# The first group's hidden activations: split where they are made, spilled in two parts, reloaded by transfers alone

## Chip, cores and metric

One core of a Trainium2 chip runs the whole program in one launch. The metric is the device time of one execution in microseconds (us); lower is better. Before the change it was measured in three runs.

## What is computed

Three layers in a row, all in float32:

```python
scores = scale * np.matmul(q, k.transpose(0, 1, 3, 2))   # 4 x 8 heads, 768 positions, 64 wide; sinks and a window of 128
a = softmax(np.where(keep, scores, -1e9))
x = np.matmul(a, v)                                      # laid out as 3072 tokens x 512
h = np.maximum(np.maximum(x @ w1, x @ w2), x @ w3)       # 512 -> 768
x2 = h @ w_out                                           # 768 -> 512
logits = x2 @ w_gate                                     # 8 experts, 384 tokens each, assigned by rank
out[mask] = np.maximum(x2[mask] @ u1[e], 0.0) @ u2[e]    # for each expert e
```

## The kernel before

TensorE gets its accuracy from splitting every float32 operand in a high part (a rounded copy, written by ScalarE) and a low part (operand minus high part, by VectorE or GpSimd), and from three products high x high, low x high, high x low. A split of one 128x384 tile is thus one ScalarE copy and one VectorE subtraction.

The 3072 tokens go through in eight groups of 384. For each group four attention units (`att`, p = 0 to 3) give the tiles `x` (128x384 each). `Moe1.group` (L260) splits them into `xh0..3`, `xl0..3` (L267, L268; one buffer each), multiplies by the three weights (L280, 36 products for each of six blocks f), takes the maximum into `hm` (L282 ScalarE, L283 VectorE; two buffers), and splits `hm` (L288, L289) into the parts of one tile `HL` (`part`, six high and six low). `Moe1.x2` (L294) multiplies H by the output weight, six accumulations of 18 products (L305), evicts (L307) and stores x2d.

The first group is an exception. When its H is made, the output weight `woh`, `wol` does not exist yet: `load_out` (L240) makes it during the second group, from six 512 KB words tiles that `single` (L214) loads into the ring `st` of the pool `conv` (two buffers), and the space of `HL` is still the landing ring of the first weights. So the first group stores `hm` itself, unsplit, into `sp` in DRAM (L285, on ScalarE's queue), and after the second group's `x2`, `reload` (L317) loads each `hm` again on SyncE's queue (L321), splits it (L323 ScalarE, L324 VectorE) into `HL`, and a second `x2` follows at once.

Program order is: group 0; group 1; x2 of group 1; reload; x2 of group 0; group 2, and so on. Attention of the coming groups is woven in at high priority, so between 177 and 233 us the engines run the two `x2` and the attention of groups 2 and 3 side by side. A scheduler that simulates the engines decides the final order on each queue; every queue then runs in order. For attention of those groups ScalarE copies keys and queries (`kh`, `qs`), evicts scores (`T`), takes exponentials (L144), rounds the probabilities (`H`, L176); VectorE does the low parts (`kz`, `qs`: L95, L97), masks (L135) and the split maxima and products; GpSimd scales (`T`, L147) and makes the low part of the probabilities (`L`, L177). Groups 0 and 1 use a simpler attention without these splits (`native`), but during group 0 the first weights are unpacked and split, on GpSimd above all (L228, L213).

Of the kernel before, what the change touches and what calls it, by code (L numbers as in the profile page):

```python
# [19 lines left out]
FT=mybir.dt.float32; FR=mybir.dt.float32r; BF=mybir.dt.bfloat16; I32=mybir.dt.int32; U8=mybir.dt.uint8; U32=mybir.dt.uint32  # L20
AF=mybir.ActivationFunctionType; OP=mybir.AluOpType; AX=mybir.AxisListType
NEG=-8.0e9
def f32(ap): return ap.bitcast(FT)
# [179 lines left out]
class Moe1:  # L203
# [56 lines left out]
    def group(s,xs,spill=None,pool=None,mid=None,between=None):  # L260

        nc=s.nc; main=s.main
        X=[]
        for p in range(4):
            h=main.tile([128,384],FR,name=f"xh{p}",bufs=1); l=main.tile([128,384],FR,name=f"xl{p}",bufs=1)
            with s.tc.high_priority():
                nc.scalar.activation(h,xs[p],AF.Copy)  # L267
                nc.vector.tensor_tensor(l,xs[p],f32(h),op=OP.subtract)  # L268
            X.append((h,l))
        H=[]  # L270
        if s.HL is None and spill is None: s.HL=main.tile([128,12,384],FR,name="HL")
        for f in range(6):
            if between is not None: between(f)
            m=main.tile([128,384],FT,name="hm",bufs=2)
            for i in range(3):
                ps=s.mm.tile([128,512],FT,name="mm")
                n=0
                for p in range(4):
                    for a,b in ((0,0),(0,1),(1,0)):
                        nc.tensor.matmul(ps[:,:384],s.W[i][a][:,p,f*128:(f+1)*128],X[p][b],start=(n==0),stop=(n==11)); n+=1  # L280
                with s.tc.high_priority():
                    if i==0: nc.scalar.activation(m,ps[:,:384],AF.Copy)  # L282
                    else: nc.vector.tensor_tensor(m,ps[:,:384],m,op=OP.max)  # L283
                if mid is not None and (f,i)==s.at: mid()
            if s.HL is None: nc.scalar.dma_start(spill[f],m); continue  # L285
            h,l=(pool.tile([128,384],FR,name=f"h{x}{f}",bufs=1) if pool else s.part(x,f) for x in "hl")
            with s.tc.high_priority():
                nc.scalar.activation(h,m,AF.Copy)  # L288
                nc.vector.tensor_tensor(l,m,f32(h),op=OP.subtract)  # L289
            if spill is not None:  # L290
                for d,x in zip(spill[f],(h,l)): nc.scalar.dma_start(d,f32(x))
            H.append((h,l))
        return H
# [21 lines left out]
                nc.scalar.activation(LG[:,t0+t,:].rearrange("p (u e) -> p u e",u=2),e,AF.Copy)  # L315
            nc.scalar.dma_start(x2d[(t0+t)*128:(t0+t+1)*128,:],o)
    def reload(s,spill):  # L317
        nc=s.nc; H=[]
        for f in range(6):
            m=s.main.tile([128,384],FT,name="hm",bufs=2)  # L320
            nc.sync.dma_start(m,spill[f])  # L321
            h,l=s.part("h",f),s.part("l",f)
            nc.scalar.activation(h,m,AF.Copy)  # L323
            nc.vector.tensor_tensor(l,m,f32(h),op=OP.subtract)  # L324
            H.append((h,l))
        return H
    def by_rows(s,spill,t0,x2d,accs,pool):

# [28 lines left out]
class Route:  # L357
# [4 lines left out]
    M=128  # L362
# [261 lines left out]
def attention_mixtures(tc,q,k,v,vs,words,wg,u1,u2,out,off=60,spread=(0,1,3,4),native=8,order='a0 a0 a0 a0 w a1 w a1 w w a1 w w a1 a2',order1='a2 o o o o o o a2 a2',back=1,at=(1,0),s1=300,s2=400,nring=6):  # L624
    nc=tc.nc
    PS=bass.MemoryType.PSUM
    with ExitStack() as ctx:
# [6 lines left out]
        x2d=dram.tile([3072,512],FT,name="x2d")  # L634
        A=Attn(tc,q,k,v,vs,consts,ac,pst,psp,pss,psv,work)
        M=Moe1(tc,words,wg,consts,wpool,main,conv,mm,pst,pss,A.ident)
        M.at=at
        LG=consts.tile([128,24,8],FT,name="LG")
        NG=8; xs={}; cnt={}
# [7 lines left out]
        with tc.block(schedule_with_timeline_sim=True):  # L647
# [16 lines left out]
            rest=None  # L664
            for g in range(NG):
                if g==1:
                    for o in order1.split(): emit(o,True)
                late=list(range(cnt.get(f'a{g+1}',-1)+1,4)) if g+1<NG else []
                def between(f):
                    if f in spread and late: late.pop(0); emit(f'a{g+1}',True)  # L670
                if g<2:
                    while late: between(spread[0])
                d = g>=NG-3
                if g==0: sp=[dram.tile([128,384],FT,name=f"sp{f}") for f in range(6)]
                if g==NG-3: sp2=[[dram.tile([128,384],FT,name=f"sp{f}{x}") for x in "hl"] for f in range(6)]
                if g==NG-1:
                    A.extra.release(); work.release(); ac.release(); psv.release(); pss.release(); psp.release()
                    acc=P("acc",1,space=PS); rc=P("rc",2,space=PS)
                    rt=P("rt",1); rw=P("rw",2); hp=A_("hp",1)
                    r=Route(tc,LG,rt,rw,rc)  # L680
                H6,H=H if g==NG-1 else None,M.group(xs[g],sp if g==0 else sp2 if g==NG-3 else None,hp if g==NG-1 else None,rest,between)
                while late: between(spread[0])
                rest=None
                if d:
                    rest=M.logits(H,3*g,LG)
                    if g==NG-1: r.bids((0,21),True)
                elif g: M.x2(H,3*g,LG,x2d)
                if g==back:
                    M.x2(M.reload(sp),0,LG,x2d)
# [30 lines left out]
            P7=[main.tile([128,384],FR,name=f"x{j}") for j in range(3)]  # L720
            for j in range(3): nc.vector.tensor_scalar(P7[j],io,r.q[:,T7+j:T7+j+1],None,op0=OP.is_equal)
        M.x2(H6,T7-3,LG,x2d,256,hp)
        M.by_rows(sp2,T7-6,x2d,acc,hp)
        with tc.high_priority(): fet(0)
        M.x2(H,T7,LG,x2d,256,hp,keep)
        hp.release()
# [62 lines left out]
```

## Time and profile before

| what | before |
|---|---|
| median of 3 runs (lowest to highest) | 992.21 us (989.67 to 995.44) |
| the profiled execution's own time | 988.75 us |
| its span | 986.9 us |
| TensorE busy (PE, share of the span) | 933.9 us (95%) |
| VectorE (DVE) / ScalarE (ACT) / GpSimd (POOL) busy | 687.5 / 534.4 / 349.0 us |

Engines are called as the profile calls them: PE is TensorE's matmuls, PEld its weight loads, DVE VectorE, ACT ScalarE, POOL GpSimd, SPq and ACTq the queues on which SyncE and ScalarE issue transfers. L305 is line 305 of the kernel before. A busy time counts the instructions of an engine, not the issue of transfers. "a <-b" behind an idle time names what ended it.

### The profile page before, as it was taken

The numbers are of one execution on the slowest core, as the hardware profiler recorded it, in microseconds if no ns is written. First come the engines' busy times: TensorE is split into PE (matmuls) and PEld (weight loads), VectorE is DVE, ScalarE is ACT, GpSimd is POOL, SyncE is SP. The second block draws the span as 40 slices with busy tenths as digits, with TensorE's granted clock in tenths as the row PEclk, the third lists the DMA queues.
The fourth block names the chain that finished last, engine by engine and source line by source line (L and its number), as shares of the span: only waits on it lengthen the run. The fifth ranks groups of instructions, "written<-read, shape, count | busy, mean of one in ns | idle before, by whom it ended". The sixth has DMA issues, their size and how long they took to land.

```text
span 986.9 us, 18459 instructions
## 1 busy us (share of the span) xinstructions
PE 933.9 (95%) x6552; PEld 853.2 (86%) x6552; DVE 687.5 (70%) x1807; ACT 534.4 (54%) x1425; POOL 349.0 (35%) x317
## 2 busy tenths in 40 slices
PE   5889999979999999999999999999999999999996
PEld 3569889969999999999999998888888888878895
DVE  4887766797889875766755335978988879774320
ACT  5766765888789786777663211333433424335431
POOL 3689256056446526415442000001303113043331
PEclk9999999979999999999999999999999999999999
DMA  7554122222112112112110002634534243454430
GB/s 231 166 187 141 50 76 67 86 91 66 39 57 83 48 34 69 40 48 88 60 44 2 1 1 87 193 112 129 164 98 168 100 158 127 136 184 145 137 107 32
DMA packets 50541, 95.03 MB, mean 96 GB/s; under 512 B 6704, under 2 KB 20784, under 8 KB 50448
## 3 DMA queue, kind: packets, MB, share of 16 engines
q1 hardware_dynamic: 40560, 71.57, 23.5%
q0 software_dynamic: 3840, 12.45, 3.6%
q10 hardware_dynamic: 6048, 9.83, 2.7%
q8 instruction: 51, 0.84, 0.4%
q14 instruction: 42, 0.34, 0.1%
HBM read 77.84 MB, written 16.12 MB: 95 GB/s over the span
## 4 chain that ended last, share of the span: by engine, by line
PE 72%; DVE 9%; issue 6%; ACT 6%; DMA 4%; POOL 2%; SPq 0%; POOLq 0%; ACTq 0%; DVEq 0%
PE mm L280 28%; PE mm L608 10%; PE acc L601 10%; PE mm L305 6%; PE po L181 3%; PE rc L406 2%; DMA sa<-in_u_dram 2%; PE pt L25 2%; PE pp L25 2%; PE po L172 1%; PE acc L336 1%; PE ps L126 1%; PE ps L127 1%; PE ps L123 1%; DVE qs L97 1%
## 5 line engine op out<-in xcount | busy, mean ns | idle before, releaser
L601 PE MATMUL acc<-wbh,HL 128*128 128x512 f32 x384 | 131.8, 400 | 0.8 <-issue 0.8
L177 POOL TENSOR_TENSOR L<-A_w,H 128x768 fp32r<-128x768 f32 x46 | 87.1, 1894 | 101.8 <-ACT H L176 95.8
L283 DVE TENSOR_TENSOR hm<-mm,hm 128x384 f32<-128x384 f32 x96 | 53.3, 555 | 68.6 <-PE mm L280 64.1
L620 POOL DMA_INDIRECT out_dram<-og,idx x24 | 31.8, 1323 | 185.8 <-ACT og L619 182.4
L305 PE MATMUL mm<-woh,HL 128*128 128x260 f32 (+1 forms) x432 | 88.2, 293 | 2.0 <-DVE HL L324 1.1
L552 ACT ACTIVATE wah<-sa 128x512 fp32r<-128x512 f32 x64 | 40.4, 632 | 89.0 <-PE mm L608 56.3
L601 PEld LDWEIGHTS acc<-wbh,HL 128*128 128x128 f32 x384 | 71.7, 189 | 14.4 <-DVE qi L520 1.3
L552 ACT ACTIVATE wbh<-sb 128x512 fp32r<-128x512 f32 x64 | 40.3, 630 | 72.4 <-PE acc L601 56.5
L601 PE MATMUL acc<-wbl,HL 128*128 128x512 f32 x192 | 77.0, 401 | 0.0
L305 PEld LDWEIGHTS mm<-woh,HL 128*128 128x128 f32 x432 | 71.1, 195 | 3.4 <-DVE HL L324 1.4
L608 PE MATMUL mm<-HL,wah 128*128 128x384 f32 x256 | 68.5, 343 | 0.0
L280 PE MATMUL mm<-xh,w0h 128*128 128x384 f32 x192 | 66.8, 348 | 1.3 <-ACT xh L267 0.6
L553 DVE TENSOR_TENSOR wbl<-sb,wbh 128x512 fp32r<-128x512 f32 x64 | 44.8, 701 | 33.0 <-ACT wbh L552 30.0
L280 PE MATMUL mm<-xh,w1h 128*128 128x384 f32 x192 | 66.8, 348 | 0.8 <-ACT hm L282 0.5
L280 PE MATMUL mm<-xl,w0h 128*128 128x384 f32 x192 | 65.5, 341 | 1.9 <-DVE xl L268 1.9
L280 PE MATMUL mm<-xh,w2h 128*128 128x384 f32 x192 | 66.4, 346 | 0.2 <-ACT hm L282 0.2
L280 PE MATMUL mm<-xh,w1l 128*128 128x384 f32 x192 | 65.3, 340 | 0.0
L280 PE MATMUL mm<-xh,w0l 128*128 128x384 f32 x192 | 65.2, 339 | 0.0
L280 PE MATMUL mm<-xl,w2h 128*128 128x384 f32 x192 | 65.1, 339 | 0.0
L280 PE MATMUL mm<-xl,w1h 128*128 128x384 f32 x192 | 65.0, 339 | 0.0
L280 PE MATMUL mm<-xh,w2l 128*128 128x384 f32 x192 | 64.8, 337 | 0.0
L612 DVE SCALAR_TENSOR_TENSOR HL<-mm,HL 128x384 fp32r<-128x384 f32 x64 | 35.4, 553 | 39.5 <-ACT HL L611 39.4
(320 smaller groups left out, 2877.2 us busy)
## 6 DMA issues: line engine op xcount, KB each, us to landing
sa<-in_u_dram SPq DMA_DIRECT2D x64, 256.0 KB
sb<-in_u_dram SPq DMA_DIRECT2D x64, 256.0 KB
HL<-in_words_dram SPq DMA_DIRECT2D x18, 512.0 KB
qn<-in_q_dram SPq DMA_DIRECT2D x24, 192.0 KB
x2d<-xo ACTq DMA_DIRECT2D x15, 256.0 KB
kn<-in_k_dram SPq DMA_DIRECT2D x12, 264.0 KB
st<-in_words_dram SPq DMA_DIRECT2D x6, 512.0 KB
vn<-in_v_dram SPq DMA_DIRECT2D x12, 256.0 KB
```

The costliest lines, as they stand in the source:

```text
L25: nc.tensor.transpose(out,x,f32(ident))
L177: nc.gpsimd.tensor_tensor(L,Af,f32(H),op=OP.subtract)
L181: nc.tensor.matmul(po[:,q:q+n],u['VS'][:,blk,128*h:128*h+128],part[:,c:c+n],start=(part is H and j==0),stop=False,skip_group_check=True)
L280: nc.tensor.matmul(ps[:,:384],s.W[i][a][:,p,f*128:(f+1)*128],X[p][b],start=(n==0),stop=(n==11)); n+=1
L283: else: nc.vector.tensor_tensor(m,ps[:,:384],m,op=OP.max)
L305: nc.tensor.matmul(ps[:,:n],H[f][a][:,t*128:(t+1)*128],s.WO[b][:,f,u,c],start=(k==0),stop=(k==17)); k+=1
L552: nc.scalar.activation(h,src,AF.Copy)
L553: (nc.gpsimd if s.n>=6 and nm=="wa" else nc.vector).tensor_tensor(l,src,f32(h),op=OP.subtract)
L601: s.mms.append(nc.tensor.matmul(acc[t],H[f][a][:,t*128:(t+1)*128],W[f][1][b],start=(f==0 and n==0),stop=(f==F-1 and n==2))); n+=1
L608: s.mms.append(nc.tensor.matmul(ps[:,:384],W[f][0][a][:,k,:],X[k][b],start=(n==0),stop=(n==11))); n+=1
L612: nc.vector.scalar_tensor_tensor(l,ps[:,:384],0.0,f32(h),op0=OP.max,op1=OP.subtract)
L620: st=nc.gpsimd.indirect_dma_start(out=s.out,out_offset=bass.IndirectOffsetOnAxis(ap=idx[:,t:t+1],axis=0),in_=o,in_offset=None)
```

## The change

The first group's H is split like that of the others, into a tile `hp` that takes turns in the ring `st` of `conv` (the same two buffers that the output weight's words land in later), and both parts are stored. `reload` has no ScalarE or VectorE work left: it loads high and low part of blocks 0 to 3 into the tiles `xh0..3`, `xl0..3`, and blocks 4 and 5 into their parts of `HL`.

```diff
@@ Moe1.group
-            if s.HL is None: nc.scalar.dma_start(spill[f],m); continue
-            h,l=(pool.tile([128,384],FR,name=f"h{x}{f}",bufs=1) if pool else s.part(x,f) for x in "hl")
+            if s.HL is None: h,l=(s.conv.tile([128,2,384],FR,name="hp",tag="st",bufs=2)[:,x] for x in range(2))
+            else: h,l=(pool.tile([128,384],FR,name=f"h{x}{f}",bufs=1) if pool else s.part(x,f) for x in "hl")
             with s.tc.high_priority():
                 nc.scalar.activation(h,m,AF.Copy)
                 nc.vector.tensor_tensor(l,m,f32(h),op=OP.subtract)
@@ Moe1.reload
-        nc=s.nc; H=[]
+        H=[]
         for f in range(6):
-            m=s.main.tile([128,384],FT,name="hm",bufs=2)
-            nc.sync.dma_start(m,spill[f])
-            h,l=s.part("h",f),s.part("l",f)
-            nc.scalar.activation(h,m,AF.Copy)
-            nc.vector.tensor_tensor(l,m,f32(h),op=OP.subtract)
-            H.append((h,l))
+            H.append([s.main.tile([128,384],FR,name=f"x{x}{f}",bufs=1) if f<4 else s.part(x,f) for x in "hl"])
+            for d,x in zip(spill[f],H[f]): s.nc.sync.dma_start(f32(x),d)
         return H
@@ attention_mixtures
-                if g==0: sp=[dram.tile([128,384],FT,name=f"sp{f}") for f in range(6)]
-                if g==NG-3: sp2=[[dram.tile([128,384],FT,name=f"sp{f}{x}") for x in "hl"] for f in range(6)]
+                if g in (0,NG-3): sp=[[dram.tile([128,384],FT,name=f"sp{g}{f}{x}") for x in "hl"] for f in range(6)]
```

The stores of both parts are the lines that stood at L290 and L291 already, on ScalarE's queue. (The sixth group's spill, `sp2` before, is only renamed.)

The scheduler then orders every queue anew. TensorE's queue where the two `x2` meet, before (`HL` is group 0's H from the first L305 here on; `kh_x`, `kz0b` are keys of group 3's attention, whose scores go to `ps`):

```order
L182 MATMUL po<-psb_105,vk_103 128x384
L126 MATMUL ps<-kh_x,qs_2602 128x260
L127 MATMUL ps<-kz1b,qs_2602 128x260
L126 MATMUL ps<-kh_x,qs_2601 128x260
L127 MATMUL ps<-kz0b,qs_2601 128x260
L305 MATMUL mm<-woh,HL 128x260
L305 MATMUL mm<-wol,HL 128x260
L305 MATMUL mm<-woh,HL 128x260
L305 MATMUL mm<-wol,HL 128x260
```

and with the change:

```order
L182 MATMUL po<-psb_105,vk_103 128x384
L126 MATMUL ps<-kh_x,qs_2634 128x260
L127 MATMUL ps<-kz1b,qs_2634 128x260
L305 MATMUL mm<-woh,xh_2291 128x260
L305 MATMUL mm<-wol,xh_2291 128x260
L305 MATMUL mm<-woh,xl_2292 128x260
L305 MATMUL mm<-woh,xh_2295 128x260
L305 MATMUL mm<-wol,xh_2295 128x260
L305 MATMUL mm<-woh,xl_2296 128x260
L305 MATMUL mm<-woh,xh_2299 128x260
```

One pair of scores has moved behind the start of group 0's `x2`, which now reads the tiles `xh`, `xl`; its first twelve products are those of blocks 0 to 3.

ScalarE's queue where group 2's x is split. Before, the first two splits (`xh_2408`, `xh_2412`) stand right behind the second group's last evictions (L282), ahead of both `x2`:

```order
L282 ACTIVATE hm<-mm 128x384
L134 ACTIVATE T_w<-ps 128x132
L256 ACTIVATE wgt<-ps 128x8
L267 ACTIVATE xh_2408<-x_986 128x384
L267 ACTIVATE xh_2412<-x_1391 128x384
L134 ACTIVATE T_w<-ps 128x132
L288 ACTIVATE HL<-hm 128x384
```

With the change they stand at the very end of group 0's `x2`, of whose twelve evictions (L307) those shown are the last two:

```order
L307 ACTIVATE xo<-mm 128x260
L144 ACTIVATE T_w,l<-T_w,m 128x132 x2
L267 ACTIVATE xh_2440<-x_986 128x384
L144 ACTIVATE T_w,l<-T_w,m 128x132 x3
L176 ACTIVATE H<-A_w 128x768
L144 ACTIVATE T_w,l<-T_w,m 128x132
L108 ACTIVATE vsp<-vn 128x4x2x64
L183 ACTIVATE x_1828<-po 64x384
L267 ACTIVATE xh_2444<-x_1427 128x384
L267 ACTIVATE xh_2448<-x_1708 128x384
L307 ACTIVATE xo<-mm 128x260
```

All four splits of group 2's x now come after the products that read the reloaded H out of the same tiles.

SyncE's queue at the reload, before and with the change:

```order
L75 DMA kn<-in_k_dram 128x528
L321 DMA hm<-sp_1032 128x384
L321 DMA hm<-sp_1033 128x384
L75 DMA kn<-in_k_dram 128x528
L77 DMA qn<-in_q_dram 128x384
L75 DMA kn<-in_k_dram 128x528
L77 DMA qn<-in_q_dram 128x384
L321 DMA hm<-sp_1034 128x384
L321 DMA hm<-sp_1035 128x384
```

```order
L321 DMA xh_2303<-sp03h 128x384
L321 DMA xl_2304<-sp03l 128x384
L75 DMA kn<-in_k_dram 128x528
L77 DMA qn<-in_q_dram 128x384
L75 DMA kn<-in_k_dram 128x528
L77 DMA qn<-in_q_dram 128x384
L321 DMA HL<-sp04h 128x384
L321 DMA HL<-sp04l 128x384
L321 DMA HL<-sp05h 128x384
L321 DMA HL<-sp05l 128x384
```

Eight transfers now come in one row ahead of the next keys, and the last four, which need the parts of `HL` that the second group's `x2` reads to its end, stand where the third and fourth transfer stood.

## Rows read from the trace of the kernel before

**Rows 1.** The page: span, busy time of each engine, PE's busy tenths in 40 slices.

```profile
span 986.9 us, 18459 instructions
...
PE 933.9 (95%) x6552; PEld 853.2 (86%) x6552; DVE 687.5 (70%) x1807; ACT 534.4 (54%) x1425; POOL 349.0 (35%) x317
...
PE   5889999979999999999999999999999999999996
```

**Rows 2.** Windows; start:end, length, busy of each engine (instructions), PEclk, DMA share, GB/s.

```profile
60.00:100.00 40.00, 38.62 (x214) 34.22 (x215) 30.03 (x54) 24.27 (x70) 35.27 (x31) 1.00 0.45 153
100.00:140.00 40.00, 38.25 (x236) 34.13 (x235) 29.98 (x64) 28.93 (x90) 15.57 (x15) 1.00 0.23 73
...
202.00:210.00 8.00, 6.85 (x37) 6.55 (x38) 7.41 (x12) 5.87 (x22) 3.63 (x2) 0.62 0.38 108
210.00:218.00 8.00, 4.15 (x25) 3.23 (x24) 7.45 (x11) 7.80 (x20) 6.15 (x5) 0.81 0.09 22
...
177.00:232.60 55.60, 47.37 (x337) 44.86 (x336) 44.48 (x83) 49.27 (x150) 20.81 (x15) 0.88 0.29 86
232.60:270.00 37.40, 37.40 (x248) 37.24 (x247) 30.62 (x61) 30.00 (x93) 19.77 (x19) 1.00 0.17 51
```

**Rows 3.** Waits of PE from 195 to 233 us: total us, times, longest.

```profile
PE ps L126 <- DVE T_w L135: 4.3, 3, 2.0
PE pp L25 <- DVE A_w L163: 1.2, 1, 1.2
PE mm L305 <- DVE HL L324: 1.1, 1, 1.1
PE pt L25 <- POOL T_w L147: 0.7, 1, 0.7
PE mm L305 <- ACT xo L307: 0.5, 1, 0.5
PE po L181 <- POOL L L177: 0.4, 1, 0.4
```

**Rows 4.** The chain that ended last, 190 to 240 us: start, us, what.

```profile
203.60 3.27 DVE HL L324 x2
206.90 2.36 DMA hm<-sp
```

**Rows 5.** Tile hm: ns min/median/max, first and last start; idle of its engine before (us, times).

```profile
L288 ACT ACTIVATE HL<-hm x12: 507/524/527, 136.5 to 292.1; 128x384 fp32r<-128x384 f32 x12
...
L285 ACTq DMA_DIRECT2D sp<-hm x6: 326/326/344, 69.4 to 118.6; - x6
...
L323 ACT ACTIVATE HL<-hm x6: 506/518/524, 192.4 to 209.3; 128x384 fp32r<-128x384 f32 x6
L324 DVE TENSOR_TENSOR HL<-hm,HL x6: 548/555/2197, 194.8 to 209.8; 128x384 fp32r<-128x384 f32 x6
...
  DMA hm<-sp: 2.0, 2
```

**Rows 6.** DVE's timeline, 180 to 240 us: start, us, instruction.

```profile
194.84 1.02 DVE L324 TENSOR_TENSOR HL<-hm,HL 128x384 fp32r<-128x384 f32 x2
...
203.51 3.36 DVE L324 TENSOR_TENSOR HL<-hm,HL 128x384 fp32r<-128x384 f32 x2
```

**Rows 7.** POOL's timeline, 170 to 240 us.

```profile
202.83 1.51 POOL L147 TENSOR_TENSOR T_x<-T_x,l 128x792 f32<-128x792 f32 x1 [4.17 <-DVE l L146]
204.29 2.16 POOL L177 TENSOR_TENSOR L<-A_w,H 128x768 fp32r<-128x768 f32 x1
```

**Rows 8.** Tile xh: the splits of x in all groups, ns min/median/max.

```profile
L267 ACT ACTIVATE xh<-x x32: 506/514/528, 32.1 to 553.6; 128x384 fp32r<-128x384 f32 x32
L268 DVE TENSOR_TENSOR xl<-x,xh x32: 546/554/1694, 32.6 to 554.6; 128x384 fp32r<-128x384 f32 x32
```

**Rows 9.** Tile st: loads and first step of the output weight's words.

```profile
L220 SPq DMA_DIRECT2D st<-in_words_dram x6: 328/356/585, 21.5 to 157.3; - x6
L226 ACT ACTIVATE st<-st x6: 653/671/687, 27.5 to 160.8; 128x512 int32<-128x512 uint32 x6
```

More of the change, by code (lines that the diff above doesn't have):

```diff
@@ L680, in attention_mixtures @@
                     r=Route(tc,LG,rt,rw,rc)
-                H6,H=H if g==NG-1 else None,M.group(xs[g],sp if g==0 else sp2 if g==NG-3 else None,hp if g==NG-1 else None,rest,between)
+                H6,H=H if g==NG-1 else None,M.group(xs[g],sp if g in (0,NG-3) else None,hp if g==NG-1 else None,rest,between)
                 while late: between(spread[0])
@@ L722, in attention_mixtures @@
         M.x2(H6,T7-3,LG,x2d,256,hp)
-        M.by_rows(sp2,T7-6,x2d,acc,hp)
+        M.by_rows(sp,T7-6,x2d,acc,hp)
         with tc.high_priority(): fet(0)
```

## The prediction

> **What bounds the kernel now.** I read the page first. TensorE is busy 933.9 of 986.9 us, so all that any change off TensorE can win is in its idle 53 us and in the stretches where its clock is down. PE's row of slices shows where: the start, the last slice, and one dip in the middle, the slice from 197 to 222 us with a 7 [rows 1]. That dip is where the second group's x2 gives way to the reloaded first group's, so it is the place of this change.
>
> The windows view sizes it. From 177.0 us, where the second group's x2 begins, to 232.6 us, where the third group's products begin, PE is busy 47.37 of 55.6 us: 8.2 us idle. [...] In the same stretch ACT is busy 49.27 us, 89%, and in the 16 us around the dip DVE is busy 7.41 and 7.45 of 8 us each [rows 2]. So it is the two feeding engines, not TensorE, that set the pace there.
>
> Who is waited for: PE waits for masks of the next attention (T_w, 4.3 us), a product A_w (1.2), the reloaded low part itself (HL of L324, 1.1), GpSimd and evictions (0.7, 0.5, 0.4): 8.2 us, the whole idle time [rows 3]. Only 1.1 us of it is a direct wait for the reload; the rest is attention that comes late because ACT and DVE also split the reloaded tiles. The chain of waits says the same: it runs through two subtractions L324 (3.27 us) and the landing of one reloaded hm (2.36 us) [rows 4].
>
> **The change, part by part.**
>
> *Removed at the reload.* Six ACT copies of 0.518 us, 3.1 us, and the 2.0 us for which ACT stood waiting for hm to land [rows 5]: 5.1 us off a queue that is 89% full. On DVE six subtractions: two in 1.02 us, two in 3.36 us [rows 6], two at the median 0.555 [rows 5], 5.5 us. What this is worth on TensorE's path no row shows. From below: nothing if attention's own chain stays as long; if ACT sets the end and its other idle time stays, 5.1 us. [...] I take 6.5 us, near ACT's end of it, because ACT remains the fullest engine (49.27 - 3.1 = 46.2 us of work against 41.7 us that TensorE would need at full clock without idle time), and a little above 5.1 since the lower clock follows the idle times and goes with them. What is late next is attention's T_w, not H: all transfers for blocks 0 to 3 can run while the second group's x2 still computes.
>
> *Transfers instead of six.* Twelve on SyncE's queue, six more issues of some 0.33 us each, as the stores on ACT's queue show [rows 5]. The eight into xh, xl wait only for the second group's last product, at 177 us; the keys queued behind them would be held that long, as they were behind the two hm before. The four into HL wait for the end of the second group's x2, then take 2.36 us each to land, overlapping; the twelve products of blocks 0 to 3 and a transposition stand ahead of them in TensorE's order. I cost them at nothing; if that cover is gone, one landing, 2.4 us.
>
> *The third group's split waits.* The tiles xh, xl are now read until the last product of the reloaded x2, so the four splits of group 2 cannot come early, as two of them did. They cost 4 x 0.514 on ACT and one 0.554 on DVE at the end of the row [rows 8], 2.6 us if TensorE stands for all of it, and nothing if the products that follow in order (three per split and weight, and the scores between) cover them. Behind the waiting copy on ACT's in-order queue stand exponentials and the rounding of H, which attention waits for. I take 1.0 us.
>
> *Added in group 0.* ACT gets six copies of 0.524 us and six more issues of 0.326 us [rows 5], 5.1 us; DVE six subtractions, 3.3 us at the median. ACT is busy 24.27 of 40 us from 60 to 100 and 28.93 of 40 from 100 to 140, DVE 30 of 40 in both; PE is idle 1.4 and 1.75 us there [rows 2]. Both engines have room, and TensorE has its own work: at the median price all is hidden. At the worst price, below, six subtractions take 6 x 2.197 = 13.2 us, 3.2 us more than the 10 us that DVE has free in the first 40. Between 0 and 3.2 I take 0.5.
>
> *The ring st.* hp occupies it during group 0, so the first two of the six 512 KB words loads leave the start (the first is at 21.5 us), with their two ACT steps of 0.671 us [rows 9]. At most 1.3 us won on ACT early; on the other side the output weight is made later, but its last first step was at 160.8 us [rows 9], 16 us ahead of its use at 177. Two loads and first steps that come later cost at most 2 x (2.36 + 0.671) = 6.1 us, with the landing of a reloaded hm [rows 4] for that of a larger tile, less than the 16. I cost it at nothing.
>
> **Sum.** -6.5 + 1.0 + 0.5 = -5.0 us. The profiled execution took 988.75 us (span 986.9), so 983.8 by its measure. That execution lies 3.5 us below the median of the three runs, 992.21; by the median the forecast is 987.2 us. About 0.5%, 5 us, is what a measurement of this kernel can tell from no change, so the forecast lies on that border.
>
> **A row against the change.** Two of the removed subtractions took 3.36 us together instead of 1.1 [rows 6], and just then GpSimd ran two operations back to back from 202.83 to 206.45 us [rows 7]. The split of x shows the same: median 0.554, at most 1.694 us [rows 8]. So the price of such a subtraction hangs on what GpSimd does. From 60 to 100 us, where most of the six now stand, GpSimd is busy 35.27 of 40 us, in the old place 20.81 of 55.6 [rows 2].
>
> [...]
>
> **The rivals.**
>
> *Absorbed.* Attention's chain is as late as before, and only ACT's 3.1 us come off, less the 1.5 us of the two costs: -1.6, 990.6 us. For it: 6.6 of the 8.2 us of waits are for attention's operands [rows 3], and PE arrives earlier at a group whose last x tile may not be there. Against it: those operands are late behind the removed work [rows 4]. That the reload's last four transfers come late (2.4 us) ends here too.
>
> [...]
>
> *Slower: the subtraction in group 0.* ACT's queue holds, right behind each copy, the issue of both stores, and the second waits for the low part. If the subtraction takes 2.197 instead of 0.555 us, ACT stands 1.64 us longer, and behind it stand the evictions (L282) of TensorE's next products and the splits of the weights. Six of these are 9.9 us; with the other two costs, 11.4 us, against a gain of 5.1 at ACT's end: +6.3, 998.5 us. For it: GpSimd's load from 60 to 100 us. Against it: ACT is idle 15.7 us of those 40. It decides when more than three of the six are stretched so and nothing covers them.
>
> **How the numbers follow.** The forecast (3.5 to 8 us faster) 0.38; TensorE full, or nearly, 0.15; absorbed 0.34; the slower rival 0.13. Of the forecast's case some four fifths lie beyond the border of 5 us or close enough to count: with the full case faster by over 0.5% is 0.45; the rest of it and the absorbed case give 0.42 within 0.5%; slower by over 0.5% 0.13. The range takes in the full case (979.8, and the 1.3 us of the start: 978.5) and, above, the absorbed case with the 2.4 us landing uncovered (993) and a little of the slower rival: 978.5 to 995.
>
> **What would show it.** Right: PE idle in the stretch between the second group's x2 and the third group's products falls from 8.2 us to some 3, the clock there rises to 0.95 or more, no L323 or L324 is left, and the busy time of ACT from 60 to 140 grows by 3.1 us with PE as busy as before. Wrong: subtractions of hp over 1 us at the median and PE waiting for hm or for weights before 140 us (slower rival); new waits of L280 for xh or xl, or for x, near 230 us as large as the old ones (absorbed); PE waiting for a transfer into HL (late reload). A change in any stretch that these steps don't name would make the sum wrong even with the right total.

## The result and the profile after

| | before | after |
|---|---|---|
| median of 9 runs each, us (lowest to highest) | 994.41 (989.67 to 996.80) | 1000.30 (997.09 to 1008.74) |
| the profiled execution, us | 988.75 | 999.37 |
| its span, us | 986.9 | 997.6 |

The ratio of the times is 1.0085, with a 95% interval from 1.0060 to 1.0111: the change made the kernel 0.85% slower, where 0.5% faster was forecast and 995.0 us was the upper end of the range.

The page of the kernel after, against [rows 1]: the dip of PE at 197 to 222 us is gone. The clock row, which before had a single 7, in that dip, has one in each of the first two slices and one from 125 to 150 us (the last line shown is the clock row of the kernel before).

```profile
span 997.6 us, 18477 instructions
...
PE 941.8 (94%) x6552; PEld 859.5 (86%) x6552; DVE 692.6 (69%) x1807; ACT 534.2 (54%) x1425; POOL 349.3 (35%) x317
...
PE   5799989899899999999999999999999999999996
...
PEclk7799979999999999999999999999999999999999
...
PEclk9999999979999999999999999999999999999999
```

To see where the time went, the program is cut where TensorE's first product of a stage starts. The windows of the kernel after (columns as in [rows 2]): groups 0 and 1, the second group's start and its rest, the two x2, group 2, and the x2 of group 2.

```profile
38.10:190.40 152.30, 143.24 (x809) 126.07 (x808) 110.46 (x215) 94.64 (x271) 91.62 (x85) 0.94 0.36 114
120.40:150.00 29.60, 24.53 (x124) 21.27 (x124) 20.82 (x42) 20.35 (x61) 12.25 (x11) 0.77 0.37 118
150.00:190.40 40.40, 39.53 (x259) 39.05 (x258) 25.36 (x54) 20.29 (x45) 20.63 (x21) 1.00 0.17 52
190.40:233.10 42.70, 40.06 (x313) 39.06 (x313) 31.26 (x57) 35.58 (x118) 15.41 (x12) 0.96 0.40 126
233.10:300.20 67.10, 62.03 (x384) 60.40 (x383) 56.42 (x107) 52.43 (x154) 36.38 (x31) 0.95 0.18 51
300.20:324.30 24.10, 22.39 (x177) 21.19 (x176) 18.60 (x39) 22.61 (x71) 11.72 (x9) 1.00 0.25 79
```

The same cut of the kernel before:

```profile
35.60:177.10 141.50, 135.80 (x799) 119.75 (x800) 103.86 (x205) 88.35 (x257) 91.56 (x86) 1.00 0.33 109
177.10:232.60 55.50, 47.27 (x336) 44.76 (x336) 44.38 (x83) 49.27 (x150) 20.81 (x15) 0.88 0.29 87
232.60:289.70 57.10, 56.45 (x372) 56.04 (x371) 46.61 (x93) 45.98 (x135) 31.70 (x30) 1.00 0.17 50
289.70:311.50 21.80, 20.83 (x171) 20.20 (x170) 20.16 (x35) 20.39 (x67) 8.68 (x7) 1.00 0.26 79
```

The first product starts 2.5 us later. Groups 0 and 1 take 10.8 us more, and as much was lost from 120.4 to 150 us alone: PE idle 5.1 us, and 24.53 us at a mean granted clock of 0.77 instead of 1, by estimate 5.6 us. The two x2 take 12.8 us less: PE idle 2.6 us, clock 0.96. That is nearly all that the stretch had lost before, by estimate 13.9 us: 8.2 us idle, and 5.7 us for 47.27 us of work at a clock of 0.88 instead of 1. But group 2 takes 10.0 us more and its x2 2.3. Together 12.8 us; what follows takes 2 us less, and the span grew by 10.7 us.

PE's instructions in brackets already say something. The x2 stretch lost 23 of its 336, and the stretches around it hold more than before: the scheduler, which orders the whole program anew, had moved attention out of the x2, so part of the 12.8 us is work that now stands elsewhere.

PE's waits from 118 to 191 us, and from 191 to 300 us, most of them new (before, the first two groups had 0.8 us for `A_w` and 0.7 for `xo`):

```profile
PE pt L25 <- POOL wol L147: 2.1, 1, 2.1
PE pp L25 <- DVE A_w L163: 1.3, 1, 1.3
PE ps L25 <- POOL cA L228: 1.0, 1, 1.0
PE ps L255 <- ACT xo L252: 0.9, 1, 0.9
...
PE mm L280 <- DVE hm L283: 2.6, 1, 2.6
PE ps L126 <- DVE T_x L135: 2.4, 1, 2.4
PE mm L280 <- ACT xh L267: 1.7, 1, 1.7
```

`ps <- cA` and `ps <- xo` are `load_out`, which makes the output weight. Against [rows 9], its first words load moved from 21.5 to 127.3 us, behind group 0's last store:

```profile
L220 SPq DMA_DIRECT2D st<-in_words_dram x6: 328/328/328, 127.3 to 165.7; - x6
```

### The profile page after: what moved, and what is told of

Same layout as the page of the kernel before. It is cut to its first block, busy times and chain, and to the rows that moved or that the text cites. A ratio compares the mean times of both kernels' runs of the same rounds, so it can differ in the third digit from the quotient of the medians.

```text
span 997.6 us, 18477 instructions
## 1 busy us (share of the span) xinstructions
PE 941.8 (94%) x6552; PEld 859.5 (86%) x6552; DVE 692.6 (69%) x1807; ACT 534.2 (54%) x1425; POOL 349.3 (35%) x317
## 4 chain that ended last, share of the span: by engine, by line
PE 66%; DVE 11%; issue 7%; ACT 7%; DMA 5%; POOL 2%; SPq 0%; POOLq 0%; ACTq 0%; DVEq 0%
PE mm L280 25%; PE mm L604 9%; PE acc L597 9%; PE mm L305 6%; PE po L181 3%; DMA sa<-in_u_dram 3%; PE rc L402 2%; PE pt L25 2%; ACT T_w L144 2%; PE pp L25 1%; PE acc L332 1%; PE po L172 1%; DVE qs L97 1%; PE ps L126 1%; PE ps L127 1%
## 5 line engine op out<-in xcount | busy, mean ns | idle before, releaser
L283 DVE TENSOR_TENSOR hm<-mm,hm 128x384 f32<-128x384 f32 x96 | 53.3, 555 | 66.7 <-PE mm L280 64.4
L305 PE MATMUL mm<-woh,HL 128*128 128x260 f32 (+1 forms) x384 | 77.7, 291 | 1.0 <-ACT xo L307 1.0
L280 PE MATMUL mm<-xh,w1h 128*128 128x384 f32 x192 | 67.1, 349 | 0.8 <-ACT hm L282 0.5
L305 PEld LDWEIGHTS mm<-woh,HL 128*128 128x128 f32 x384 | 62.5, 192 | 2.0 <-ACT xo L307 1.4
L163 DVE TENSOR_TENSOR A_w<-pp,ul 128x768 f32<-128x768 f32 x54 | 51.4, 952 | 17.2 <-PE pp L25 15.0
```

The costliest lines, as they stand in the source:

```text
L163: nc.vector.tensor_tensor(A,pt[:,:384].rearrange("p (i q) -> p i q",q=128)[:,:,None,:].to_broadcast([128,3,2,128]), s.ul[:,None,:,:].to_br ...
L305: nc.tensor.matmul(ps[:,:n],H[f][a][:,t*128:(t+1)*128],s.WO[b][:,f,u,c],start=(k==0),stop=(k==17)); k+=1
```

## The experiments

Four theories, numbered as the expectations have them (they call the scheduler the planner). **1**: ring `st`, held by `hp` through group 0, makes the output weight late. **2**: `xh` and `xl`, read until the last product of the reloaded x2, make group 2's splits late. **3**: attention's own pace sets the time from the x2 on, so that work taken from it there wins nothing. **4**: the removed work is worth its price, and the loss comes from the order that the scheduler makes of the changed program.

**Parts of the change, in the scheduler's order.** hp_elsewhere takes `hp` out of the ring; the two spare tiles of 384 floats lie in `woh`, `wol`, which attention uses as scratch until `load_out` (the line that hands this space over is left out here):

```diff
-h,l=(s.conv.tile([128,2,384],FR,name="hp",tag="st",bufs=2)[:,x] for x in range(2))
+h,l=(s.spare.tile([128,384],FR,tag="hp"+x) for x in "hl")
```

> The two parts of group 0's H stand in floats that attention leaves unused inside woh and wol, not in ring st; the reload into xh and xl stays. Theory 1 (ring st held by group 0 keeps the output weight's loads behind its last store, so that the work of load_out and attention meet in group 1): the first two st loads leave before 30 us again, the second group's products take 56 to 59 us instead of 70.0, and its clock is 1.00; group 2 keeps its 69 us, since the split of x still waits. Total 985 to 991 us, some 11 us under the change. Rival (the work taken out of the two x2 has to stand somewhere, and ACT and DVE lack room wherever it goes): group 1 stays at 67 us or more, total within 3 us of the change (997 to 1003).

ring_only goes the other way, from the kernel before:

```diff
-m=main.tile([128,384],FT,name="hm",bufs=2)
+m=main.tile([128,384],FT,name="hm",bufs=2) if s.HL is not None else s.conv.tile([128,384],FT,name="hm0",tag="st",bufs=2)
```

> The kernel before, with one thing of the change alone: hm of group 0 is a tile of ring st; spill whole, reload and split as before. Theory 1: the st loads leave after group 0's last store, group 1 takes 66 to 72 us instead of 56.3 with a clock near 0.8 at its start, total 1000 to 1006 us, 8 to 12 above before. Rival (the split of H that was moved, or the reload, made the loss): group 1 within 3 us of 56.3, total within 4 us of before (990 to 998).

reload_to_HL changes the target alone, and both_elsewhere joins it with hp_elsewhere:

```diff
-H.append([s.main.tile([128,384],FR,name=f"x{x}{f}",bufs=1) if f<4 else s.part(x,f) for x in "hl"])
+H.append([s.part(x,f) for x in "hl"])
```

> The changed kernel, with all twelve reloaded parts in HL and none in xh and xl. Theory 2 (tiles xh and xl held until the last product of the reloaded x2 make the splits of group 2 late, and these make its stalls and its lower clock): the splits run before 225 us as before, group 2 takes 57 to 60 us instead of 69.4; the reloaded x2 starts by one landing later, up to 3 us. Total 988 to 993. Rival (attention moved out of the two x2 fills group 2, whatever tile is used): group 2 stays at 66 us or more, total 999 to 1003.

> Both edits: the parts of group 0 in the unused floats of woh and wol, the reload all into HL. Theories 1 and 2 together: group 1 at 56 to 59, the two x2 at 43 to 48, group 2 at 57 to 60, total 977 to 985 us, 9 to 17 under before, and the fastest of the four. If the work only moves: within 3 us of before (991 to 997) or slower.

All four came out slower than before, and none had a lower ratio than the change. Lengths are from first product to first product, us, in the one execution of each kernel that was profiled. Such an execution can lie some us from the median of its kernel's runs (before 5.7 below, kept_both_behind, further down, 3.9 above), so lengths say where time went, and the ratios what it came to:

| kernel | ratio to before (95%) | groups 0, 1 | two x2 | group 2 |
|---|---|---|---|---|
| before | 1 | 141.5 | 55.5 | 57.1 |
| after | 1.0085 (1.0060 to 1.0111) | 152.3 | 42.7 | 67.1 |
| hp_elsewhere | 1.0115 (1.0067 to 1.0163) | 145.1 | 43.6 | 68.3 |
| ring_only | 1.0217 (1.0161 to 1.0273) | 147.5 | 55.9 | 58.4 |
| reload_to_HL | 1.0154 (1.0102 to 1.0206) | 150.5 | 46.7 | 62.0 |
| both_elsewhere | 1.0124 (1.0060 to 1.0188) | 147.9 | 46.4 | 64.4 |

The named stages moved the way theories 1 and 2 say (group 1 alone takes 56.3 us before and 70.0 after; it fell to 58.6 with `hp` elsewhere and is 66.4 with the ring alone; group 2 fell by 5.1 with the reload in `HL`), and the total did not follow. The loss came up in stages that the edit does not touch. In hp_elsewhere the x2 of group 3 takes 27.8 us instead of 20.8; 4.3 us of that are one wait in attention's scores, and the mean granted clock of the stage is 0.82 instead of 1.00:

```profile
PE ps L126 <- DVE T_x L135: 4.3, 1, 4.3
```

**Nothing to split at all, and the order alone.** no_split bounds the gain from above: the split of the reloaded H is done nowhere.

```diff
-m=s.main.tile([128,384],FT,name="hm",bufs=2)
-nc.sync.dma_start(m,spill[f])
 h,l=s.part("h",f),s.part("l",f)
-nc.scalar.activation(h,m,AF.Copy)
-nc.vector.tensor_tensor(l,m,f32(h),op=OP.subtract)
+for x in (h,l): nc.sync.dma_start(f32(x),spill[f])
```

> The kernel before, with the split of the reloaded H left out: twelve transfers bring the whole H into both the high and the low part (six copies and six subtractions are not done anywhere, so the output is not the reference's). This is the most that the removed work can give. What the prediction held: the two x2 shrink from 55.5 to some 43 to 49 us and the total falls with them, 979 to 988 us. Theory 3, from the attention tiles: group 2 cannot go on before the twelfth attention tile, which is done at 233.0 us before and between 233 and 242 in every run so far, whatever the x2 took; so the x2 shrinks by 5 to 12 us and group 2 and what follows give 5 to 12 back: total 990 to 1002, no faster than before.

It gave 1.0015 (0.9983 to 1.0047). The two x2 fell from 55.5 to 46.2 us, and group 3 started 7.3 us earlier than at 311.5; the products of groups 5 to 7 started at 450.0 instead of 453.0 us, and the stage after them at 599.7 instead of 599.2. In this execution, the fastest of its ten (988.3 us, their median is 996.1), the gain was there and was given back. other_order_only changes no work (`off=56` for `off=60`):

> The kernel before with attention's priority offset 56 instead of 60: the same instructions, moved a little against each other on every engine. If the order that the planner happens to find is worth much by itself, the total moves by 4 us or more either way with no work changed; if it is not, it stays within 3 us of before (991 to 997).

It gave 1.0071 (1.0040 to 1.0102): the order alone is worth as much as the whole change. loads_first_before and loads_first_elsewhere emit `load_out` first (`'o o o o o o a2 a2 a2'` for `'a2 o o o o o o a2 a2'`):

> The kernel before with the six load_out ahead of the third group's first attention tile instead of behind it (the order of emission alone). Theory 3: what counts is when load_out ends, since tiles 11 and 12 of attention wait for the space that the words ring leaves; here the last part of the output weight is done before 165 us instead of 175, the keys of tile 11 are loaded by 162 instead of 170, tile 12 is done before 229, total 984 to 992. Rival: attention starts later by the same amount, total within 3 us of before or slower.

> The parts of group 0's H in the unused floats of woh and wol, the reload into xh and xl, and load_out ahead of the third group's first attention tile. Theory 3: load_out ends before 170 us (184.4 with hp_elsewhere), tile 12 before 230 instead of 238.1, group 2 falls from 68.3 to some 58 us, total 983 to 993, 12 to 20 under hp_elsewhere. Rival (the reload into xh and xl alone costs group 2 its 12 us): group 2 stays above 64, total 1000 or more.

1.0069 (1.0045 to 1.0092) and 1.0044 (1.0011 to 1.0077). `load_out` did end earlier, but attention's tenth tile moved behind it and took the time that was won: with the order of emission I had moved a whole tile. The second of them bears on theory 3. Its windows, the two x2 and the start of group 2:

```profile
174.70:212.90 38.20, 37.85 (x316) 37.42 (x315) 28.70 (x55) 35.96 (x113) 18.23 (x13) 1.00 0.44 138
212.90:230.00 17.10, 12.13 (x66) 10.98 (x65) 15.51 (x25) 13.70 (x41) 8.28 (x8) 0.84 0.24 73
```

The two x2 ran at full clock with 0.35 us idle, in 38.2 us; then group 2 started 13 us before its last x tile (the twelfth) was ready at 226.1 us (before, that tile is ready at 233.0 us and group 2 starts at 232.6). PE lost 5 us there at once, 3.6 of them waiting for attention and 1.4 for the low part of x.

**The order kept.** To take the scheduler out, the kernels named kept_... hold every instruction that the kernel before has too in that kernel's place on its engine: a list of its order, and a dependency without a semaphore from each instruction to the next one of its engine (the code is shortened here). In the trace of kept_no_split the instructions of PE, DVE, ACT and POOL come in the order of the kernel before through its first 600 us, but for those that are left out. What an edit adds is placed by the scheduler. The instructions pass through a helper, so all rows of these kernels have line L36.

```diff
+for eng,seq in rows.items():
+    for i in (tap.seen[k] for k in seq if k in tap.seen):
+        if last is not None: tc.add_manual_dep(i,last.name,NoSync,reason="order kept")
+        last=i
```

> As no_split (the split of the reloaded H is left out, so the output is not the reference's), but every instruction that the kernel before has too stands in that kernel's order on its engine (written down as a list and held by dependencies within an engine, which cost no semaphore). Theory 4 (the removed work is worth what the prediction said, and the loss comes from the order that the planner makes of the changed program): the two x2 shrink from 55.5 to 44 to 49 us and nothing is given back; group 3 starts 6 to 11 us earlier than at 311.5 and the total is 984 to 989, 5 to 10 under before. Theory 3 (attention's own pace sets the time from 177 us on, in any order): within 3 us of before.

> As both_elsewhere (parts of group 0's H in the unused floats of woh and wol, reload into HL), in the order of the kernel before. Theory 4: some 2 us less than kept_no_split wins, since the split now stands in group 0: 985 to 991, 3 to 9 under before, and 14 or more under the same edits in the planner's order (1006.2). Theory 3: within 3 us of before. If the split in group 0 is what costs: over 997 and group 0 longer than 86 us.

> As hp_elsewhere (reload into xh and xl), in the order of the kernel before but for the four splits of group 2's x, which must follow the reloaded x2. Against kept_both_elsewhere this tells what the tiles xh and xl cost: the reload need not wait for the first x2, but the splits come late. Theory 2 (late splits hold up group 2): 3 to 6 us more than kept_both_elsewhere, group 2 61 us or more. Rival: the same within 2 us, group 2 at 57 to 59.

> The changed kernel itself, parts of group 0 in ring st and reload into xh and xl, in the order of the kernel before but for the words loads of the output weight with their first ACT step, and the four splits of group 2's x, which cannot keep their places. Against kept_hp_elsewhere this is ring st alone. Theory 1: group 1 takes 62 to 68 us with a clock under 0.95 at its start, 5 to 10 us more in total than kept_hp_elsewhere. Rival (the ring cost nothing, as I predicted, and group 1's 70.0 us were the planner's order): within 2 us of kept_hp_elsewhere, group 1 under 60.

| kernel | ratio to before (95%) | groups 0, 1 | two x2 | group 2 |
|---|---|---|---|---|
| kept_no_split | 0.9995 (0.9970 to 1.0020) | 142.5 | 54.8 | 56.4 |
| kept_both_elsewhere | 1.0027 (1.0006 to 1.0048) | 146.1 | 56.0 | 56.6 |
| kept_hp_elsewhere | 1.0027 (1.0009 to 1.0045) | 147.1 | 51.0 | 59.8 |
| kept_change | 1.0054 (1.0033 to 1.0076) | 149.2 | 52.1 | 59.7 |

Theory 4 is right in its second half: both_elsewhere and hp_elsewhere lose 0.97 and 0.88 points of their ratios (a point is 0.01, 1% of the time before) when only the order goes back. Its first half falls: even with no split anywhere, and nothing reordered, the two x2 take 54.8 us. In total kept_no_split and kept_both_elsewhere lie within 3 us of before, where theory 3 had them.

The trace of kept_no_split shows one reason. SyncE's queue there:

```profile
192.74 0.33 SPq L36 DMA_DIRECT2D kn<-in_k_dram  x1
193.94 5.83 SPq L36 DMA_DIRECT2D HL<-sp  x12
199.92 0.33 SPq L36 DMA_DIRECT2D qn<-in_q_dram  x1
```

Before, those queries went ahead of the reload:

```profile
192.66 0.33 SPq L77 DMA_DIRECT2D qn<-in_q_dram  x1
195.43 0.80 SPq L321 DMA_DIRECT2D hm<-sp  x2
```

Now they stand behind twelve transfers, which take 6.0 us of the queue, 5.83 us of it from the first issue to the end of the last. The wait for `HL` ahead of the first is 0.9 us at most. Counted from the first product of the x2, the queries go at 20.8 us instead of 15.6, 5.3 us later. ACT's in-order queue waits for them, and behind it TensorE for the masks of the scores (ACT's timeline and PE's waits in kept_no_split):

```profile
203.85 0.52 ACT L36 ACTIVATE qs<-qn 64x384 fp32r<-64x384 f32 x1 [3.83 <-DMA qn<-in_q_dram]
```

```profile
PE ps L36 <- DVE T_w L36: 6.3, 3, 4.4
```

Ring `st` is seen by itself between kept_hp_elsewhere and kept_change, which differ by it and by the places of the words loads. The first two words loads, which went at 22.4 and 24.0 us in kept_hp_elsewhere, go at 127.0 and 131.1 us in kept_change, the second after a wait of 3.8 us for group 0's last store. PE waits 3.1 us for the first unpacked words there, and GpSimd, which unpacks them, had stood 6.9 us (PE's waits in group 1, GpSimd's timeline, and the window over group 1's start):

```profile
PE ps L36 <- POOL cA L36: 3.1, 1, 3.1
```

```profile
133.37 1.61 POOL L36 TENSOR_TENSOR cA<-cA,st 128x512 int32<-128x512 int32 x1 [6.93 <-DVE cA L36]
```

```profile
125.70:145.00 19.30, 14.69 (x74) 13.12 (x73) 12.40 (x24) 13.76 (x38) 8.87 (x8) 0.82 0.47 152
```

The same stretch of kept_hp_elsewhere has 2.8 us more of PE's work in it:

```profile
125.80:145.00 19.20, 17.46 (x93) 15.56 (x92) 13.61 (x26) 14.02 (x39) 10.04 (x7) 0.82 0.31 98
```

The clock, 0.82 in both, does not tell them apart. Theory 1 holds at some 3 us, less than the 5 to 10 expected; the wait is plain in the trace, while the ratios differ by 0.27 points, no more than their uncertainty. Theory 2 holds for group 2: it takes 59.8 us with the reload in `xh`, `xl` and 56.6 with it in `HL`, and PE waits 1.8 us for `xl`. But the two x2 are 5.0 us shorter, so that these two kernels come out the same. One reason is SyncE's queue again. With `xh`, `xl` as targets eight of the transfers are issued around the first product of the x2 and the last four behind the queries. These queries go 15.5 us after that product (at 184.7 us) in kept_hp_elsewhere, and 15.6 in kept_change and in the kernel before:

```profile
200.20 0.33 SPq L36 DMA_DIRECT2D qn<-in_q_dram  x1
```

So, with the order kept, the held queries belong to a reload that goes all into `HL`, and not to the change.

**The transfers behind the queries, and which engine pays in group 0.** One line (shortened) moves all twelve transfers to the place of the third load of hm. kept_both_no_sub also leaves the subtractions out.

```diff
-ks=[(eng,c,x,j)]
+ks=[(eng,c,x,j)] if (eng,c,x,j)!=third_hm_load else reload_transfers
```

> As kept_no_split (no split of the reloaded H anywhere, so the output is not the reference's), with the twelve transfers in SyncE's queue where the third load of hm stood before, behind the queries (qn) that went at 192.7 us there. If the removed work was on the path and only the queue hid it: ACT's idle 3.8 us for qn and TensorE's 4.4 us for T_w go, the two x2 take 46 to 51 us instead of 54.8 (55.5 before), total 985 to 990, 0.993 to 0.998 of before. If attention's chain holds TensorE anyway: x2 at 53 or more, total within 2 us of before.

> As kept_both_elsewhere with the transfers behind those queries. The x2 falls from 56.0 by the same 4 to 8 us as in kept_no_split_behind; groups 0 and 1 keep their 146 us (142.5 without the split). Total 988 to 993, no faster than before by more than 0.5% and 3 to 6 us under kept_both_elsewhere. It would be the version of the change that is no slower than the kernel before.

> As kept_both_behind without the six subtractions of group 0 (the high part is stored twice, so the output is not the reference's). If VectorE pays for the split in group 0 (its subtractions stand among attention's masks, one took 4.25 us): groups 0 and 1 fall from 146 to 142 to 143 us and the wait for T_w of 1.4 to 1.9 us goes. If ACT pays (six copies and six more issues of stores): they stay at 145 to 147.

| kernel | ratio to before (95%) | groups 0, 1 | two x2 | group 2 |
|---|---|---|---|---|
| kept_no_split_behind | 0.9966 (0.9941 to 0.9992) | 143.0 | 52.6 | 56.6 |
| kept_both_behind | 0.9982 (0.9958 to 1.0006) | 147.5 | 52.6 | 56.6 |
| kept_both_no_sub | 0.9987 (0.9958 to 1.0016) | 143.3 | 52.3 | 56.6 |
| kept_both_last_on_gpsimd | 0.9996 (0.9964 to 1.0029) | 145.7 | 52.2 | 56.6 |

The x2 fell by 2.2 and 3.4 us, less than the 4 to 8 expected, but kept_no_split_behind is the first kernel here that is faster than before: work removed altogether, in the old order, with the queue clear, is worth 0.34% (0.08 to 0.59). In kept_no_split_behind PE is still idle for 6.4 us, where it was 8.2, and it waits for other links of the same chain (the window of the two x2, and PE's waits in it):

```profile
181.10:233.70 52.60, 46.25 (x337) 44.23 (x336) 39.95 (x78) 47.23 (x147) 20.61 (x15) 0.90 0.37 118
```

```profile
PE ps L36 <- DVE T_w L36: 2.1, 2, 1.7
PE pp L36 <- DVE A_w L36: 1.6, 1, 1.6
PE mm L36 <- ACT T_w L36: 1.1, 1, 1.1
```

What the split costs in group 0 is not settled. The profiled executions say 4.2 us, all VectorE's (147.5 with the subtractions, 143.3 without); the times do not show it (990.71 and 990.77 us; the profiled execution of kept_both_behind is 3.9 us above its median). Yet the profiles agree among themselves: groups 0 and 1 take 141.5 to 143.3 us in the four executions without the subtractions (before, kept_no_split, kept_no_split_behind, kept_both_no_sub) and 146.1 to 149.2 in the four kept kernels with all six. The place is the start of group 1. Its first 9.2 us and the 10 us behind them, in kept_both_no_sub and then in kept_both_behind, and the wait that grew there (same order):

```profile
124.70:133.90 9.20, 8.51 (x55) 7.21 (x53) 8.95 (x17) 8.40 (x26) 3.40 (x3) 1.00 0.42 140
133.90:143.90 10.00, 8.96 (x57) 8.47 (x56) 4.88 (x12) 6.22 (x16) 6.40 (x4) 1.00 0.17 55
...
127.30:136.50 9.20, 8.03 (x52) 6.76 (x51) 8.98 (x17) 7.80 (x23) 3.74 (x4) 1.00 0.38 122
136.50:146.50 10.00, 8.88 (x49) 8.36 (x48) 4.95 (x11) 6.65 (x18) 6.38 (x4) 0.83 0.22 76
```

```profile
PE ps L36 <- ACT xo L36: 0.7, 1, 0.7
...
PE ps L36 <- ACT xo L36: 1.2, 1, 1.2
```

All four executions without the subtractions have 8.51 us of PE's work in the first window, a wait of 0.7 us and a clock of 1.00 in the second; the kept kernels with them have at most 8.05 us, waits of 1.1 to 1.5 us and a clock of 0.66 to 0.83. One last attempt moved the subtractions of blocks 4 and 5 to GpSimd:

```diff
-nc.vector.tensor_tensor(l,m,f32(h),op=OP.subtract)
+(nc.gpsimd if s.HL is None and f>=4 else nc.vector).tensor_tensor(l,m,f32(h),op=OP.subtract)
```

> As kept_both_behind, with the low parts of group 0's blocks 4 and 5 made by GpSimd instead of VectorE. If it is the place in VectorE's queue that costs: groups 0 and 1 fall from 147.5 to 143 to 145 us, the clock from 130 to 150 us stays at 1.00, total 986 to 989, 0.994 to 0.997 of before and faster than both kernels. If a GpSimd subtraction holds VectorE up in its turn, or holds up P's normalisation behind it: 147 or more, total as kept_both_behind (990.7) or slower.

Groups 0 and 1 fell by 1.8 us in its profile, short of the expected range and little more than the 1.4 us between kept_both_behind and kept_both_elsewhere, which are alike up to there. The clock behind the start of group 1 is 0.83 again, and the time is that of the kernel before. No version of the change that computes the whole result beat the kernel before.

## Why the prediction was wrong

One way through the kernels that were measured leads from the kernel before to the change in these steps. Beside the ratios stands the length from the first product to group 3 in the profiled execution (275.9 us before):

| step | kernel | ratio | step, points | length, us | step, us |
|---|---|---|---|---|---|
| the removed work, order kept, queue clear | kept_no_split_behind | 0.9966 | -0.34 | 274.0 | -1.9 |
| the split in group 0 | kept_both_behind | 0.9982 | +0.16 | 278.5 | +4.5 |
| reload into `xh`, `xl` instead of `HL` | kept_hp_elsewhere | 1.0027 | +0.45 | 279.7 | +1.2 |
| ring `st` | kept_change | 1.0054 | +0.27 | 282.9 | +3.2 |
| the scheduler's order of the rest | after | 1.0085 | +0.31 | 286.2 | +3.3 |

A step of the ratios is uncertain by some 0.3 points and a length is that of one execution. Clear of that are a gain, smaller than forecast (0.08 to 0.59 points, where 0.65 were forecast), and the costs behind it of 1.2 points together (0.9966 to 1.0085), where 0.15 were forecast. How the costs share out is less sure: the ratios and the lengths agree for the last two steps, and not for the second and third.

**Removed at the reload: -6.5 us; measured -3.4.** The step that failed is that ACT's 5.1 us come off the path because ACT is 89% busy. The stretch is bound by one attention unit after the other, each a chain of key and query loads, rounding, scores, masks and products across all engines; ACT is busy with it, but what TensorE waits for is the chain, as the waits that are left in kept_no_split_behind show. Taking 3.1 us of copies and 5.5 us of subtractions away moved the x2 by 3 us. "What is late next is attention's T_w" was right and should have set the size. The lower end of the range, with its 979.8 us, takes off this stretch the whole 13.9 us that it had lost; no run shows that gain: with the order held the two x2 fell by 4.5 us at most (51.0 in kept_hp_elsewhere). As signs I had given an idle time near 3 us and a clock of 0.95 in that stretch: both came true (2.6 us, 0.96) and proved nothing, because attention had been moved out of the stretch.

**Transfers instead of six: 0; not shown wrong.** The prediction says that the keys queued behind the eight transfers would be held "as they were behind the two hm before". With the order kept that is so: the keys and the queries go as long after the first product of the x2 as before, and no wait for a transfer into `HL` shows. The price stands in the other target: with all twelve in `HL`, ahead of the queries, 0.45 points (kept_both_elsewhere against kept_both_behind).

**The ring st: 0; measured +0.27 points, a wait of 3.1 us.** The 16 us in hand were counted at the end of the work, at the last words. The wait came at the front: the first unpacked words are what TensorE's in-order queue wants early in group 1, and their loads now go only when group 0 is done. The bound of 6.1 us was right, the slack that was to hide it lay elsewhere.

**The third group's split waits: +1.0, bounds 0 to 2.6.** Group 2 takes 3.2 us more (59.8 against 56.6), above the upper bound, and the x2 1.6 us less than in kept_both_behind (51.0 against 52.6), a gain that the sum had not. The ratios give 0.45 points for the two together, more than the lengths; what the rest of it is stays open.

**Added in group 0: +0.5, bounds 0 to 3.2.** The times give 0.16 points, 1.6 us, uncertain by more than that; the lengths give 4.5 us, above the bound. The term is too small by the profiles and not shown wrong by the times. What the profiles show is what the slower rival had named, in small: an eviction on ACT's queue that TensorE waits for comes later, and only with the subtractions. Its price of 9.9 us is not reached.

**What no step had: the order.** Every engine's order is made anew from the whole changed program. The prediction read its waits from the old order and treated them as places of the kernel. An edit of one constant cost 0.71%; the same two sets of edits cost 1.15 and 1.24% in the scheduler's order and 0.27% in the old one. None of the nine programs in an order of the scheduler's own was faster than the kernel before; what makes that one order better was not studied. For the change itself the step is 0.31 points, at the edge of what the runs can tell.

Of the rivals, *Absorbed* had the right mechanism for the x2 (attention's chain as late as before; its gain of 3.1 us at ACT stands beside 3.4 measured). The slower rival had the place in group 0. None had the wait for the ring or the order.

The row against the change stands behind the slower rival: the subtractions moved to the place with most GpSimd work should lengthen. The trace agrees for each of the six. The four that ran beside GpSimd's operations, from 72.76 to 100.80 us, took 0.91 to 1.45 us, and the two that ran beside none, at 110.90 and 125.94 us, took 0.56 and 0.55. It agrees by the median too, 0.954 us after against 0.555 for L324 [rows 5], but not by the sum: the six take 5.5 us in all before and 5.6 after, because two of L324 had been long already.

```profile
L289 DVE TENSOR_TENSOR hp<-hm,hp x6: 545/954/1452, 72.8 to 125.9; 128x384 fp32r<-128x384 f32 x6
```

So the row against the change found next to nothing more to pay for in their sum. Group 0 took 82.3 us after and 85.2 before, but with 431 products of PE in it instead of 449, since the scheduler had moved some; these two lengths say nothing about the split.

## What to carry to other kernels

Where a scheduler orders the whole program, measure an edit twice: as it comes out, and with the old order held; the difference is the order, and it can be larger than the edit (in both_elsewhere 0.97 points, against 0.27 for its edits). Busy time taken from a nearly full engine is worth what the next link of the chain behind it allows (here 3.4 us for 3.1 us of copies and 5.5 us of subtractions), so follow that link before putting a price on it. And a buffer lent to a new user, or a row of transfers put into an in-order queue, costs at the first thing that stands behind it, not at the last (here a wait of 3.1 us for the first unpacked words, and queries held for 5.3 us).

## What was not expected of the hardware

With the order held, the stages behind the edits repeat to a few tenths: group 3 takes 50.3 to 50.4 us in all eight kept kernels and in the kernel before, and the x2 behind it 20.8. The start does not: the first product of group 0 comes at 35.6 us before, 36.6 in kept_no_split and 38.1 in kept_no_split_behind, with the same instructions up to there. A difference of 2 us between two profiles is nothing if it lies in the start.

A short idle time can cost twice. In kept_hp_elsewhere PE was idle 1.15 us, and the next 10 us ran at a mean granted clock of 0.66, by estimate 3 us more (9.41 us of work, a third of the clock missing); in the kernel before, 0.7 and 1.1 us of idle time in the same two places left the clock at 1.00, and kept_both_behind, with 1.17 us, got 0.83. In the kernel before the products show a lower clock one by one: behind a wait of 2.00 us those of L305 start 0.22 us apart, and 0.12 us apart some 7 us later. The two windows of kept_hp_elsewhere, then PE's timeline of the kernel before:

```profile
125.80:135.00 9.20, 8.05 (x52) 6.77 (x52) 8.98 (x17) 7.84 (x24) 3.66 (x3) 1.00 0.39 127
135.00:145.00 10.00, 9.41 (x43) 8.79 (x42) 4.63 (x10) 6.18 (x17) 6.38 (x4) 0.66 0.23 72
...
201.99 0.58 PE L126 MATMUL ps<-kh_x,qs 128*128 128x260 f32 x1 [2.00 <-DVE T_w L135]
202.37 0.42 PE L127 MATMUL ps<-kz0b,qs 128*128 128x260 f32 x1
202.59 0.42 PE L305 MATMUL mm<-woh,HL 128*128 128x260 f32 x1
202.80 0.42 PE L305 MATMUL mm<-wol,HL 128*128 128x260 f32 x1
203.02 0.42 PE L305 MATMUL mm<-woh,HL 128*128 128x260 f32 x1
...
209.62 0.28 PE L305 MATMUL mm<-woh,HL 128*128 128x260 f32 x1
209.74 0.28 PE L305 MATMUL mm<-wol,HL 128*128 128x260 f32 x1
209.86 0.28 PE L305 MATMUL mm<-woh,HL 128*128 128x260 f32 x1
```

And one subtraction of a 128x384 tile took 4.25 us instead of 0.55 while GpSimd ran without a gap, three operations of 1.3 us in that time (shown below, VectorE and GpSimd in kept_hp_elsewhere). A GpSimd without a gap does not give that length by itself: in the kernel after, the subtraction at 95.07 us took 1.45 us, and GpSimd had no gap there either, from 93.16 to 97.68 us.

```profile
73.30 4.25 DVE L36 TENSOR_TENSOR wol<-hm,woh 128x384 fp32r<-128x384 f32 x1
...
73.37 1.29 POOL L36 TENSOR_TENSOR cA<-cA,HL 128x512 int32<-128x512 int32 x1
74.63 1.27 POOL L36 TENSOR_TENSOR w2l<-HL,w2h 128x512 fp32r<-128x512 f32 x1
75.86 1.26 POOL L36 TENSOR_TENSOR w0l<-cA,w0h 128x512 fp32r<-128x512 f32 x1
```
